# Hand-set TensorE order, V mixed a batch ahead, in-place channel results and GpSimd sorts in a fused attention and MLP kernel

## The chip, the cores and the metric

The kernel runs on one core of a Trainium2 chip. The metric is the time of one execution in microseconds (us), by the device's clock; several executions are timed and the median is given. A run is "fast" or "slow" by a simple rule: on one core it is called slow when it is more than 1.5% above the fastest of the same kernel. A ratio is the mean time of one kernel's fast runs over the mean of the other's fast runs of the same rounds, so it isn't quite the ratio of the medians quoted beside it.

The engines are TensorE (PE in the profile; its weight loads are PEld), VectorE (DVE), ScalarE (ACT), GpSimd (POOL) and SyncE (SP). In this kernel GpSimd issues the loads from DRAM, beside some elementwise work, and SyncE issues the stores, the V round trip through DRAM and the DMA transposes. In the traces here each of them works through its instructions in order: below, TensorE stands 7.5 us at one matmul with other work behind it.

## The reference, cut to what matters

Shapes: q, k, v are 4 batches x 8 heads x 768 x 64; the MLP's width is 512, hidden width 2048.

```python
P = sort_net                                  # (B, H, 8, 8)
for _ in range(5):                            # normalise rows, then columns
    P = exp(P - max(P)); P = P / sum_rows(P); P = P / sum_cols(P)
k_sorted = einsum('bhij,bhjcd->bhicd', P, k_blocks)   # "mixing" of K: 8 blocks of 96 rows
v_sorted = einsum('bhij,bhjcd->bhicd', P, v_blocks)   # "mixing" of V
x = softmax(q_b @ k_sorted_b^T / 8) @ v_sorted_b      # attention inside each block
a1  = alpha1 * x + beta1
tok = einsum('ts,bsd->btd', w_tok, a1)        # token mixing, 768 x 768
u   = x + lam * tok
ch  = relu((alpha2 * u + beta2) @ w_ch1) @ w_ch2      # hidden layer, then channel layer
out = u + lam * ch
```

## The kernel before

Per batch the kernel mixes K and V, does attention, the token layer (`tok`), the hidden layer (`h`) and the channel layer (`ch`). The MLP of one batch and the attention of the next are interleaved on TensorE. A scheduler sets the order of an engine's instructions unless `fixed` is set; `bufs` says how many copies of a tile exist. V takes a round trip: TensorE mixes it, the result is written to DRAM (`vscr`) and read back regrouped (`Vs`). W1 and W2 are the two MLP weights.

```python
# loads, issued by GpSimd (cut)
def load_weights():
    for g in range(4): pool.dma_start(W1p[...g...], w1v[...g...])
    load_raw(1, 1)                                    # V of batch 1
    for g in range(4): pool.dma_start(W2p[...g...], w2v[...g...])
...
def sort_wtok(n):                                     # regroups columns of w_tok
    for lo, hi, base in ((0, 96, 0), (96, 128, TAIL)):
        dve.tensor_copy(t_[:, :, :, lo:hi], wt16[...])
...
def emit_scores(b, h4, g, spins=0):                   # eight matmuls, then one exp
    sps = psa([128, 2, 4, 128], FT, "sc_ps")
    ...
def moe_ch(b, hf, kks=range(3)):
    ost = att.tile([128, C], FT, name="ost", tag="ost", bufs=2)
    ...
    dve.tensor_tensor(cps[:], cps[:], lamB[:, lo:hi], ALU.mult)
    dve.tensor_tensor(ost[:, lo:hi], cps[:], u_of[b][kt][:, lo:hi], ALU.add)
    nc.sync.dma_start(out[...], ost[...])
...
pool.tensor_copy(gate[:], Vs[1][0:1, 0, 0:2])         # "the Vs gate": GpSimd waits here
load_raw(2, 1)                                        # V of batch 2
load_raw(2, 0)                                        # K of batch 2
pool.fixed = False
...
for b in range(1, B):
    if b > 1:
        ...
        mixing_matrices(b); mix_v(b)                  # V of the batch itself
        ...
        mix_k(b)
    emit_attention(b)
    moe_h(b - 1, 0); moe_ch(b - 1, 0); moe_h(b - 1, 1) # (b > 1)
    moe_a(b)                                          # token layer and transposes of u
    moe_ch(b - 1, 1)
    if b == 1: load_q(2); cross_q(2)                  # q of batch 2 and its DMA transposes
```

The softmax here doesn't subtract the row's maximum and nothing guards it: scores larger than these inputs give would overflow.

## Time and profile before

| | before |
|---|---|
| median of the first 3 runs | 269.15 us (268.52 to 269.49); with a fourth, used in the comparison below, 268.94 |
| span of the profiled run | 266.8 us |
| TensorE busy | 257.6 us, 97% |
| first token matmul of batches 0, 1, 2, 3 | 34.1, 85.4, 144.2, 203.0 us |

The first lines are from the page of the profiled run: each engine's busy time, and (in 40 slices of the span) TensorE's busy tenths.

```profile
span 266.8 us, 5149 instructions
...
PE 257.6 (97%) x2049; PEld 141.6 (53%) x2059; DVE 154.8 (58%) x333; ACT 125.8 (47%) x232; POOL 92.5 (35%) x100
...
PE   7799999999999999999999999999999999999993
```

TensorE hardly idles from the second slice on, and the next view gives it the full clock (1.00) in every stretch. That view sums up stretches cut at the token layers; its columns are the stretch, its length, then busy time (and number of instructions) of PE, PEld, DVE, ACT and POOL, the granted clock, the DMA share and GB/s.

```profile
34.10:85.42 51.32, 51.12 (x442) 29.28 (x443) 36.38 (x72) 30.96 (x58) 26.77 (x28) 1.00 1.28 187
85.42:144.19 58.77, 58.46 (x418) 30.75 (x419) 35.10 (x71) 28.25 (x52) 25.52 (x25) 1.00 0.91 130
144.19:202.97 58.78, 58.47 (x419) 30.76 (x419) 35.11 (x71) 28.24 (x52) 16.42 (x13) 1.00 0.42 70
202.97:266.80 63.83, 59.53 (x321) 30.94 (x322) 22.84 (x40) 19.91 (x39) 4.00 (x4) 1.00 0.19 50
```

Two equal periods of 58.8 us stand between the token layers of batches 1, 2 and 3. In the chain of waits (start, length, what) one place in such a period isn't TensorE:

```profile
109.28 0.62 PE k_ps L65 x8
...
109.92 0.58 ACT kT L65
...
111.70 0.58 ACT kT L65
...
112.30 0.50 ACT hTa L65
```

Four evictions of mixed K on ScalarE, of which the first and the last are shown, hold the chain for 2.4 us. TensorE has other work meanwhile (a whole run of hidden matmuls), so most of it is hidden; "on the chain" means here only that the next hidden matmul group got its buffer from there.

### The profile page before, as it was taken

The page shows a single profiled execution, that of the slowest core. Times are in us where ns is not written, and L with a number is a line of the kernel's source. Part 1 is how long each engine was busy: PE and PEld are TensorE (multiplying, and loading weights), DVE is VectorE, ACT ScalarE, POOL GpSimd, SP SyncE. Part 2 cuts the span into 40 slices and gives each one's busy share as a digit, 9 for nine tenths or more (in the row PEclk, how much of TensorE's full clock was granted, in tenths as well). Part 3 has the DMA queues.
Part 4 walks back from the last instruction along what each step waited for, and adds up shares of the span by engine and source line. Part 5 has one row for each costly group of instructions (what it writes and reads, how often), then busy time and mean ns, then how long its engine had stood idle before and what let it go on. Part 6 is the DMA issues. An engine that isn't in the chain of part 4 may idle for free.

```text
span 266.8 us, 5149 instructions
## 1 busy us (share of the span) xinstructions
PE 257.6 (97%) x2049; PEld 141.6 (53%) x2059; DVE 154.8 (58%) x333; ACT 125.8 (47%) x232; POOL 92.5 (35%) x100
## 2 busy tenths in 40 slices
PE   7799999999999999999999999999999999999993
PEld 2467745565565444554565444554565445545542
DVE  5878788629567966722585966704675962042033
ACT  3376757643585312980375404970474305504600
POOL 8524689203575615007917225002409000000000
PEclk9999999999999999999999999999999999999999
DMA  6999999999999544499996342494200432012012
GB/s 83 174 208 251 207 210 207 211 216 112 211 157 155 113 84 117 114 82 89 202 211 136 61 100 80 118 98 62 80 2 2 81 76 79 2 39 79 2 39 79
DMA packets 62423, 30.88 MB, mean 116 GB/s; under 512 B 48888, under 2 KB 58112, under 8 KB 62400
## 3 DMA queue, kind: packets, MB, share of 16 engines
q0 software_dynamic: 23024, 15.60, 39.4%
q1 hardware_dynamic: 39280, 14.89, 32.6%
q8 instruction: 16, 0.26, 0.4%
q14 instruction: 7, 0.06, 0.1%
q10 hardware_dynamic: 96, 0.07, 0.1%
HBM read 32.78 MB, written 8.65 MB: 155 GB/s over the span
## 4 chain that ended last, share of the span: by engine, by line
PE 89%; ACT 4%; DVE 4%; issue 1%; DMA 1%; DVEq 0%; ACTq 0%
PE ch_ps L65 31%; PE h_ps L65 30%; PE tok_ps L65 12%; PE x_ps L65 5%; PE sc_ps L65 4%; ACT kT L65 2%; PE v_ps L65 2%; PE k_ps L65 1%; PE q_ps L65 1%; ACT et L65 1%; DVE csum L65 1%; DVE P L65 1%; PE m_ps L65 1%; DVE rsum L65 1%; DMA P<-in_sort_net_dram 1%
## 5 line engine op out<-in xcount | busy, mean ns | idle before, releaser
L65 PE MATMUL h_ps<-a2T,W1p 128*128 128x384 bf16 x512 | 93.4, 326 | 0.1
L65 ACT ACTIVATE hTa<-h_ps 128x384 bf16<-128x384 f32 x96 | 45.9, 492 | 68.1 <-PE h_ps L65 67.0
L65 PE MATMUL ch_ps<-W2p,hTa 128*128 128x512 bf16 (+2 forms) x290 | 65.9, 370 | 0.5
L65 PEld LDWEIGHTS <-W1p 128*128 128x128 bf16 x512 | 47.5, 98 | 30.3 <-issue 0.9
L65 DVE TENSOR_TENSOR ch_ps<-ch_ps,lamB 128x512 f32<-128x512 f32 (+2 forms) x25 | 16.9, 676 | 63.2 <-PE ch_ps L65 60.5
L65 POOL TENSOR_SCALAR u<-b1lB,rs 128x512 f32<-128x512 f32 x18 | 28.8, 1610 | 64.1 <-DVE ost L65 59.3
L65 PEld LDWEIGHTS <-hTa 128*128 128x128 bf16 x300 | 28.7, 98 | 32.4
L65 PE MATMUL tok_ps<-x,w_tokT 128*128 128x512 f16 x144 | 32.1, 379 | 0.0
L65 POOL TENSOR_TENSOR u<-x,u 128x512 f32<-128x512 f16 x22 | 25.3, 1181 | 18.1 <-DVE x L65 17.3
L65 ACT ACTIVATE et<-sc_ps 96x768 f16<-96x768 f32 x32 | 24.9, 807 | 11.7 <-PE sc_ps L65 11.7
L65 ACT CAST u<-u 128x512 f16<-128x512 f32 x24 | 14.8, 618 | 24.8 <-DVE u L65 24.8
L65 PE MATMUL ch_ps<-W2p,hTb 128*128 128x512 bf16 (+2 forms) x100 | 25.0, 371 | 0.0
L65 PEld LDWEIGHTS <-w_tokT 128*128 128x128 f16 x180 | 14.8, 97 | 16.1
L65 DVE TENSOR_TENSOR tok_ps<-tok_ps,a1lB 128x512 f32<-128x512 f32 x24 | 16.5, 692 | 7.3 <-PE tok_ps L65 7.3
L65 DVE CAST kT<-k_ps 64x512 f16<-64x512 f32 x24 | 16.5, 688 | 3.4 <-PE k_ps L65 3.0
L65 DVE TENSOR_TENSOR x<-x_ps,recip 96x512 f16<-96x512 f32 (+2 forms) x32 | 17.6, 554 | 0.9
L65 DVE TENSOR_TENSOR u<-tok_ps,u 128x512 f32<-128x512 f32 x24 | 16.4, 688 | 1.7
L65 ACT ACTIVATE hTb<-h_ps 128x384 bf16<-128x384 f32 x32 | 15.3, 497 | 3.8 <-PE h_ps L65 3.4
L65 DVE TENSOR_TENSOR ost<-ch_ps,u 128x512 f32<-128x512 f32 (+2 forms) x25 | 16.6, 665 | 0.6
L65 POOL DMA_DIRECT2D qn<-in_q_dram x18 | 15.5, 875 | 4.2 <-PE q_ps L65 3.4
L65 PEld LDWEIGHTS <-hTb 128*128 128x128 bf16 x100 | 9.6, 98 | 10.9
L65 PEld LDWEIGHTS <-et 96*128 96x128 f16 (+2 forms) x288 | 12.4, 99 | 4.6 <-issue 1.2
(95 smaller groups left out, 214.7 us busy)
## 6 DMA issues: line engine op xcount, KB each, us to landing
out_dram<-ost SPq DMA_DIRECT2D x23, 192.0 KB, 2.2
raw<-in_v_dram POOLq DMA_DIRECT2D x8, 384.0 KB, 8.9
raw<-in_k_dram POOLq DMA_DIRECT2D x8, 384.0 KB, 10.9
vscr<-vA SPq DMA_DIRECT2D x6, 384.0 KB, 4.4
Vs<-vscr SPq DMA_DIRECT2D x6, 384.0 KB, 7.7
W1p<-in_moe_w_ch_dram POOLq DMA_DIRECT2D x4, 512.0 KB, 10.1
W2p<-in_moe_w_ch_dram POOLq DMA_DIRECT2D x4, 512.0 KB, 17.9
qn<-in_q_dram POOLq DMA_DIRECT2D x12, 128.0 KB, 5.8
```

The lines of the kernel that those rows point to most:

```text
L65: ins = getattr(self.eng, name)(*args, **kwargs)
```

## The change

The intent: (1) from batch 1 TensorE's order is written out, with score groups in pairs and each attention step set after a stated amount of hidden and channel work; (2) V of batch b+1 is mixed during batch b; (3) the channel result is added into `u` in place, which frees memory; (4) the column sorts of w_tok go from VectorE to GpSimd; and the start of batch 0 is regrouped. With it the order of the loads changes. The core of the diff, with cuts:

```diff
 def sort_wtok(n):
-            dve.tensor_copy(
+            pool.tensor_copy(
                 t_[:, :, :, lo:hi], ...
... in moe_ch
-                dve.tensor_tensor(ost[:, lo:hi], cps[:], u_of[b][kt][:, lo:hi], ALU.add)
-                nc.sync.dma_start(out[...], ost[...])
+                dve.tensor_tensor(u32[:, lo:hi], cps[:], u32[:, lo:hi], ALU.add)
+                nc.sync.dma_start(out[...], u32[...])
... loads of batch 0 and 1
+    load_w1(range(2)); load_raw(1, 1)
+    for n in range(3):
+        sort_wtok(n)                      # GpSimd waits for w_tok here
+    load_w1(range(2, 3)); prep_affine(); load_raw(1, 0); load_w1(range(3, 4)); load_q(1)
...
+    load_w2(range(2))                     # first half of W2
...
-    pool.tensor_copy(gate[:], Vs[1][0:1, 0, 0:2])
-    load_raw(2, 1)
-    load_raw(2, 0)
-    pool.fixed = False
+    pool.tensor_copy(gate[32:64, :], Vs[1][32:64, 0, 0:2])
+    load_q(2)
+    load_w2(range(2, 4))                  # second half of W2, behind the gate
+    load_raw(2, 1)
+    load_raw(2, 0)
+    cross_q(2, regroup[1])                # six DMA transposes of q
+    moe_rows(1, range(5))
+    pe.fixed = True
...
     for b in range(1, B):
+        if b == 1:
+            fill = chain(moe_h(0, 1), moe_ch(0, 0), moe_ch(0, 1, (0,)))
+            steps = ...attention_steps(1, 3.0, 0.3)
+        else:
+            fill = chain(moe_h(b - 1, 0), moe_ch(b - 1, 0), moe_h(b - 1, 1), moe_ch(b - 1, 1, (0,)))
+            steps = ...mix_k..., attention_steps(b, 5.3)
+        if b < B - 1:                     # V of the next batch
+            steps[at:at] = [(g, lambda n=n: mixes(b + 1, n)) ...]
+        weave(fill, steps)                # a step follows so many us of fill
+        moe_a(b)
+        run(moe_ch(b - 1, 1, (1, 2)))
+        if b < B - 1:
+            moe_rows(b + 1, range(3))
+        if b == 1:
+            load_q(3); load_raw(3, 1); load_raw(3, 0); cross_q(3, turned[-1])
```

## The prediction

> **What bounds the kernel.** TensorE. The page gives PE 97% busy of 266.8 us, and the chain of waits is 89% PE. Busy is not issue time, so I read starts in that view: 64 hidden-layer matmuls (384 columns) take 10.40 us, 162.5 ns each; 36 token matmuls (512 columns) 7.77 us, 216 ns. That is N/2.4 GHz plus about 2.5 ns, as the Trainium skill states ("TensorE: Matmul & The Clock Gate", "Wait, 56ns, not 53.3ns?"), so these runs have no slack. By the chain, in stages:
> - 0 to 12 us: normalising P (DVE/ACT chain), TensorE spinning.
> - 12 to 34: batch 0 attention and turning w_tok; first token matmul at 34.1.
> - 34 to 55: token, hidden and V mixing of batch 0, nearly dense.
> - 55 to 93: batch 1. Then two equal periods of 58.8 us (93.4, 152.2, 211.0), then a dense 52 us to 262.4 and a 4 us tail.
>
> **A 58.8 us period.** Hidden, channel and token matmuls need 20.8 + 20.7 + 7.8 = 49.3 us, mixing V and K 2.8. Scores and values plus stalls take the other 6.7. Before runs eight score groups of eight matmuls (0.31 us each, of which about 0.13 is the switch out of it, plus 0.09 going in) and TensorE stands still 0.1 to 0.3 us at some hidden or score groups (timeline: K evictions of 4 x 0.58 us on ACT hold the chain).
>
> **What the change does.**
> 1. Fixed TensorE order with paired score groups (four of sixteen) placed among channel/hidden units so each evacuation is covered. It should save about 0.23 x 4 us of switching plus half of the stalls: 1.5 us in each of the two periods, 1 us in batch 1. The dense end is unchanged.
> 2. V mixed a batch ahead: mostly moved work (1.3 us a batch stays); it takes the Vs round trip through DRAM (4.4 + 7.7 us to land) off the start of each batch. Included in 1.
> 3. In-place channel result: same two DVE operations; frees memory for two hidden tiles and eleven u tiles. No time of its own.
> 4. Batch 0: K before V, q issued before the identity, ten spin matmuls in the attention removed, w_tok evictions split over ACT and DVE. Scores start near 14.5 instead of 17.8 us. But w_tok still lands near 22.5 (before: GpSimd's W1 issue waited for it until 23.06), and the sorts now follow it on GpSimd: DVE took 0.45 + 0.48 us per sort. GpSimd's cost for such a strided copy isn't in this trace; it takes 2.7 cycles per element for tensor_tensor. The skill ("GPSIMD Engine Reference", "Engine selection") calls one-input operations "roughly line-rate", no run yet shows it: estimate 1.3 to 2.6 us per sort, all three done at 27 to 31. ACT then needs six evictions of about 0.65 us. I expect the first token matmul at 31 to 33: 1 to 3 us gained, not the 4 that earlier scores would give.
>
> Sum: 1.5 + 1.5 + 1 + 2 + 0.5 (batch 0's MLP) = 6.5 us. All on the TensorE chain.
>
> **Prediction: 262.6 us, 8 in 10 between 258.5 and 266.5.** Faster by over 2%: 0.66; within 2%: 0.31; slower: 0.03.
>
> **Right if** the first token matmul is at 31 to 33 us, periods are about 57.3 us, score groups show as sixteen. **Wrong if** a GpSimd sort takes over 3.5 us (first token matmul at 35 or later); if the fixed order now waits in batch 1 for late loads (q of batch 1, W2's second half, V of batch 2), as W1, W2 and q were moved behind the sorts and the Vs gate; or if exp, evictions and relu saturate ACT where scores lie within hidden units. If w_tok sorting is cheap, the gain could reach 9 us.

## More of the kernel before

GpSimd's loads, in order of time (start, length of issuing, engine, operation, what, count, idle time before it and what ended it):

```profile
27.31 1.54 POOL L65 DMA_DIRECT2D W2p<-in_moe_w_ch_dram  x2
29.09 0.75 POOL L65 DMA_DIRECT2D W2p<-in_moe_w_ch_dram  x1 [0.24 <-DMA W1p<-in_moe_w_ch_dram]
31.60 0.74 POOL L65 DMA_DIRECT2D W2p<-in_moe_w_ch_dram  x1 [1.76 <-DMA W1p<-in_moe_w_ch_dram]
```

So all of W2 is issued by 31.6 us. By the completion counts in the trace it has landed by 50.2 us, and the channel layer first needs it at 55.2.

## The result, and the profile after

The changed kernel takes 279.4 us (median of 4 runs, 277.96 to 281.36) against 268.94 us before: ratio 1.0392, 95% interval 1.032 to 1.0465. It is 3.9% slower. The same lines of the page of the changed kernel:

```profile
span 279.6 us, 5126 instructions
...
PE 254.3 (91%) x2047; PEld 141.0 (50%) x2047; DVE 143.7 (51%) x313; ACT 138.6 (50%) x251; POOL 92.4 (33%) x100
...
PE   5988899999710999999999999999999999999994
...
PEclk9999899999975799999999999999999999999999
```

There is a hole at slices 11 to 13 (about 75 to 91 us) where TensorE is nearly idle, and the granted clock drops to half around it and once before, at slice 5. The stretches, cut at the token layers as before:

```profile
32.37:106.75 74.38, 59.68 (x467) 32.11 (x466) 34.38 (x70) 38.00 (x68) 28.26 (x32) 0.89 1.25 153
106.75:163.63 56.88, 56.53 (x420) 30.79 (x418) 32.46 (x62) 31.89 (x57) 23.87 (x23) 1.00 1.12 138
163.63:219.38 55.75, 55.39 (x414) 30.23 (x412) 31.75 (x62) 28.84 (x54) 16.08 (x13) 1.00 0.18 44
219.38:279.60 60.22, 56.24 (x309) 29.33 (x306) 22.84 (x40) 19.39 (x38) 5.96 (x6) 0.99 0.20 53
```

The two later periods went from 58.8 to 56.9 and 55.8 us; the stretch of batch 1 went from 51.3 to 74.4. Two pieces of work moved into that stretch from later ones: a third of a channel half (16 matmuls at 216 ns, 3.45 us, from the end) and one V mixing (6 x 216 ns, 1.3 us, out of the third period). That explains 4.75 of the 23.1 us. Most of the rest is told by TensorE's waits (what waited, for what: us in total, times, longest):

```profile
PE ch_ps L65 <- DMA W2p<-in_moe_w_ch_dram: 11.0, 2, 7.5
PE v_ps L65 <- DMA raw<-in_v_dram: 3.1, 1, 3.1
```

In the list of waits of the kernel before, no DMA appears for TensorE. In order of time:

```profile
75.06 0.38 PE L65 MATMUL ch_ps<-W2p,hT 128*128 128x512 bf16 x1
78.94 1.02 PE L65 MATMUL ch_ps<-W2p,hT 128*128 128x512 bf16 x4 [3.49 <-DMA W2p<-in_moe_w_ch_dram]
87.45 0.58 PE L65 MATMUL ch_ps<-W2p,hT 128*128 128x512 bf16 x1 [7.49 <-DMA W2p<-in_moe_w_ch_dram]
91.08 1.01 PE L65 MATMUL v_ps<-raw,bigV 128*128 128x512 f16 x2 [3.05 <-DMA raw<-in_v_dram]
```

TensorE runs one channel matmul at 75.06, then stands for the third and the fourth quarter of W2 and for V of batch 2: 3.5 + 7.5 + 3.1 = 14.0 us. While it stands the clock falls to half from 80.7 to 94.3 us (the trace's clock record). So the 23.1 us are 4.75 of moved work, 14.0 of stops, an estimated 1.6 for the work done at half clock from 91.1 to 94.3 us, 1.7 for another half-clock stretch at 32.9 us (see b2), and about 1 us that isn't accounted for. Why these loads are late, GpSimd shows:

```profile
24.64 4.67 POOL L65 COPY wtp<-wt 128x1152 f16<-128x1152 f16 x6 [6.39 <-DMA wt<-in_moe_w_tok_dram]
...
63.02 0.18 POOL L65 COPY gate<-Vs 32x2 f16<-32x2 f16 x1 [21.20 <-DMA Vs<-vscr]
63.62 5.26 POOL L65 DMA_DIRECT2D qn<-in_q_dram  x6 [0.42 <-issue]
68.82 1.55 POOL L65 DMA_DIRECT2D W2p<-in_moe_w_ch_dram  x2
70.29 1.16 POOL L65 DMA_DIRECT2D raw<-in_v_dram  x2
```

GpSimd's sorts took 4.67 us in all, well inside the estimate. But at the gate it waited 21.2 us until V of batch 1 had come back from DRAM, then issued q of batch 2, which is needed at about 134 us, and only then the second half of W2, needed at 75 us, and V of batch 2, needed soon after that. And beside these loads SyncE runs the six DMA transposes of that same q. A DMA transpose, undisturbed and queued one after another, starts 1.3 us after the one before it in the kernel before (first fence; one of the six came late because its u did); in the changed kernel (second fence) six hold SyncE for 24.5 us, of which only 0.4 us is waiting for q:

```profile
90.37 8.90 SPq L601 DMA_TRANSPOSE a2T<-u  x6
```

```profile
67.24 24.53 SPq L140 DMA_TRANSPOSE qT<-qn  x6
```

The loads suffer too: between 80 and 86 us all DMA together moved 98 GB/s. In e2 below, with the same loads and no transposes beside them, it moved 183 GB/s (69 to 77 us), so it isn't simply that more bytes had to be moved.

The kernel before had such an overlap as well, later on and with nobody waiting: five transposes of q of batch 3 beside loads of q, V and K took 12.9 us, where five of batch 2 had taken 7.2 us.

```profile
128.79 12.89 SPq L149 DMA_TRANSPOSE qT<-qn  x5
```

### The profile page after: what moved, and what is told of

It is laid out like the page before. It is cut to its first block, busy times and chain, and to the rows that moved or that the text cites. A ratio compares the mean times of both kernels' runs of the same rounds, so it can differ in the third digit from the quotient of the medians.

```text
span 279.6 us, 5126 instructions
## 1 busy us (share of the span) xinstructions
PE 254.3 (91%) x2047; PEld 141.0 (50%) x2047; DVE 143.7 (51%) x313; ACT 138.6 (50%) x251; POOL 92.4 (33%) x100
## 4 chain that ended last, share of the span: by engine, by line
PE 67%; DMA 20%; POOL 6%; ACT 3%; DVE 1%; issue 1%; SPq 0%; POOLq 0%; DVEq 0%
PE ch_ps L65 29%; PE h_ps L65 21%; PE tok_ps L65 11%; DMA raw<-in_v_dram 7%; DMA wt<-in_moe_w_tok_dram 6%; DMA Vs<-vscr 4%; DMA vscr<-vA 3%; POOL qn L65 2%; PE x_ps L65 2%; PE v_ps L65 2%; ACT kT L65 2%; PE sc_ps L65 2%; POOL wtp L65 2%; POOL raw L65 1%; ACT hT L65 1%
## 5 line engine op out<-in xcount | busy, mean ns | idle before, releaser
L65 PE MATMUL ch_ps<-W2p,hT 128*128 128x512 bf16 (+2 forms) x400 | 89.0, 374 | 11.0 <-DMA W2p<-in_moe_w_ch_dram 11.0
L65 PE MATMUL h_ps<-a2T,W1p 128*128 128x384 bf16 x512 | 89.5, 326 | 1.4 <-ACT hT L65 0.7
L65 ACT ACTIVATE hT<-h_ps 128x384 bf16<-128x384 f32 x128 | 60.3, 493 | 53.4 <-PE h_ps L65 53.0
L65 PEld LDWEIGHTS <-hT 128*128 128x128 bf16 x400 | 38.0, 99 | 46.0 <-issue 5.4
L65 DVE TENSOR_TENSOR ch_ps<-ch_ps,lamB 128x512 f32<-128x512 f32 (+2 forms) x25 | 16.9, 676 | 74.1 <-PE ch_ps L65 51.4
L65 PE MATMUL tok_ps<-x,w_tokT 128*128 128x512 f16 x144 | 33.9, 393 | 0.0
L65 ACT CAST u<-u 128x512 f16<-128x512 f32 x24 | 14.7, 618 | 28.0 <-DVE u L65 28.0
L65 DVE RECIPROCAL recip<-x_ps 96x8 f32<-96x8 f32 (+1 forms) x32 | 6.2, 195 | 28.8 <-PE x_ps L65 28.8
L65 ACT CAST vA<-v_ps 128x1024 f16<-128x1024 f32 x8 | 8.1, 1010 | 21.5 <-PE v_ps L65 21.5
L65 DVE TENSOR_TENSOR u<-ch_ps,u 128x512 f32<-128x512 f32 (+2 forms) x25 | 16.7, 667 | 0.8
L65 PEld LDWEIGHTS <-et 96*128 96x128 f16 (+1 forms) x288 | 12.1, 105 | 2.3
L65 PE MATMUL x_ps<-Vs,et 96*128 96x65 f16 (+1 forms) x288 | 12.6, 197 | 0.0
## 6 DMA issues: line engine op xcount, KB each, us to landing
W2p<-in_moe_w_ch_dram POOLq DMA_DIRECT2D x4, 512.0 KB, 13.3
```

What stands on the lines that cost most here:

```text
L65: ins = getattr(self.eng, name)(*args, **kwargs)
```

## The experiments

Theories, as they stood after reading the traces. A: loads that miss a deadline. B: GpSimd's sorts push all later loads back. C: the hand-set order costs time in itself. D: DMA transposes and loads that run side by side slow each other. E: mixing V a batch ahead, which moves a deadline forward, is the main cost. Every kernel below gave correct outputs. "Landing" is read from the completion counts of a DMA in the trace.

### e1: all of W2 early

```diff
     moe_start(0)
-    load_w2(range(2))
+    load_w2(range(4))
...
     load_q(2)
-    load_w2(range(2, 4))
     load_raw(2, 1)
```

> Only edit to the changed kernel: the second half of W2 is issued together with the first half (at about 41 us), not behind GpSimd's wait for Vs of batch 1. Theory A (late loads: what GpSimd issues behind the Vs gate at 63 us misses its deadline, and a hand-set TensorE order turns that into a stop): both W2 waits (3.5 and 7.5 us) vanish, only a wait for V of batch 2 at about 77 us remains, no longer than 5 us; time 266 to 271 us. Theory B (GpSimd sorts are to blame) and theory C (the hand-set order itself costs time everywhere): little moves, above 276 us.

Measured: 275.41 us (273.04 to 277.38), ratio 1.02 (1.0138 to 1.0262), outside the range I gave. The W2 waits are gone, as theory A has it. But the profile, which fell on the run that counts as slow (277.38), has two V waits:

```profile
PE v_ps L65 <- DMA raw<-in_v_dram: 7.3, 2, 4.2
```

The first, 4.2 us, is V of batch 2 as expected. The second is V of batch 3, at 130 us: in the changed kernel the earlier stop had hidden that it is late too. While it was loaded, SyncE again ran transposes of q:

```profile
120.59 16.85 SPq L140 DMA_TRANSPOSE qT<-qn  x3
```

Three transposes took 16.9 us. So a delay taken away early turned up again at the next deadline, and taking away 11.0 us of W2 waits bought about 5 us (from 3.9% to 2.0% over the kernel before, fast runs).

### e2: the transposes of q of batch 2 a phase later

```diff
     load_raw(2, 0)
-    cross_q(2, regroup[1])
...
         if b == 1:
+            cross_q(2, turned[-1])
             load_q(3)
```

> Only edit: the six DMA transposes of q of batch 2, which run from 67 to 92 us beside the late loads and are not needed before about 134 us, are issued after the transposes of u of batch 1. If they choke the loads (theory D): W2's second half lands by about 80 and V of batch 2 by about 83 us instead of 87 and 91, time 269 to 274 us. If the loads are only late because they are issued late (theory A alone): landing times move by less than 2 us, time above 277 us.

Measured: 288.38 us (283.29 to 291.1; two of the four runs count as slow), ratio of the fast runs 1.0745. The landing times moved as theory D said: W2's last quarter at 77.6 instead of 87.4 us, V of batch 2 at 81.3 instead of 90.9 (2.4 us of it because the gate opened earlier). From issue to landing the last W2 quarter took 10.4 us instead of 17.8. But the time got worse: q of batch 3 has to wait for the transposes of q of batch 2 (they share a buffer), V of batch 3 stands behind q of batch 3 in GpSimd's queue, and TensorE stood 9.6 us for it (and 3.0 us for W2):

```profile
PE v_ps L65 <- DMA raw<-in_v_dram: 13.1, 2, 9.6
```

So D is supported by the landings; that the whole loss lies in this place is not.

### e3: sorts on VectorE, each before its pair of transposes

```diff
-            pool.tensor_copy(
+            dve.tensor_copy(
                 t_[:, :, :, lo:hi], ...
-    for n in range(3):
-        sort_wtok(n)
     load_w1(range(2, 3))
...
+    sort_wtok(0)
     prep_wtok(range(0, 2))
     pv0(3, 0)
+    sort_wtok(1)
     prep_wtok(range(2, 4))
     ...
```

> Only edit: the three sorts of w_tok run on VectorE again (each just before its pair of transposes), so GpSimd's queue never waits for w_tok. Theory B (GpSimd sorts delay all later loads and so cause the stop): the stop in batch 1 shrinks by over 6 us and the time is below 273 us. Theory A: the DMA queue was never empty until 55 us, so loads land as before; only the first token matmul comes 1 to 2.5 us earlier and the half-clock stretch at 33 us may go; time 275 to 279 us.

Measured: 283.18 us (280.7 to 288.61), ratio 1.0487: a miss, in the direction against theory B. The first token matmul came at 40.1 us instead of 32.2, since sort, transposes, evictions and the next sort had become one serial chain:

```profile
PE wtok_ps L65 <- DVE wtp L65: 5.1, 3, 2.2
PE ch_ps L65 <- DMA W2p<-in_moe_w_ch_dram: 3.9, 2, 3.6
```

W1's third quarter, which stood behind the sorts, was issued 5 us sooner and landed no sooner (38.8 instead of 38.0 us): the DMA queues had been busy all the time. The last quarter of W2 and V of batch 2 landed no sooner either (87.8 and 91.8 us instead of 87.4 and 90.9). With 3.5 us for V the stops in batch 1 came to 7.4 us instead of 14.0, a fall that theory B had asked for; but from the token layer on TensorE's work came 7.8 us later here, and that alone brings it closer to loads that land as before.

### e5: V mixed in its own batch

```diff
-        if b < B - 1:
-            at = len(steps) - (3 if b == 1 else 6)
-            steps[at:at] = [(g, lambda n=n: mixes(b + 1, n)) ...]
...
+            steps = [(g, lambda n=n: mixes(b, n)) for n, g in enumerate((0.6, 0.7, 1.1))]
```

> Only edit: V of batches 2 and 3 is mixed at the start of its own batch, no longer a batch ahead. If the V deadline moved ahead is the main cause (theory E): time 268 us or less. Theory A: the W2 waits stay (W2's second half still lands at 79 and 87 us), only the 3 us wait for V goes: 274 to 278 us.

Measured: 295.31 us (293.32 to 297.42), ratio 1.0969: far outside what I expected, and slower than the changed kernel. The W2 waits stayed (5.8 us) and the V wait went, as A has it, but the later batches now waited for the Vs round trip (4.0 us in batch 2) and, with the fill used up, for VectorE before the token layer (6.1 us in two waits). The edit changed where the fill ends as well, so it doesn't measure V's mixing ahead by itself. It shows no sign that E is the main cause. But E has a part in the V wait: before, TensorE first reads V of batch 2 at 106 us, in the changed kernel it would at about 77.

### b1: loads in the order of their deadlines

All W2 at 41 us; behind the gate V and K of batch 2, then q; V and K of batch 3 after the rows of u; transposes of q a phase later.

```diff
-    load_q(2)
-    load_w2(range(2, 4))
     load_raw(2, 1)
     load_raw(2, 0)
-    cross_q(2, regroup[1])
+    load_q(2)
     moe_rows(1, range(5))
+    load_raw(3, 1)
+    load_raw(3, 0)
...
         if b == 1:
-            load_q(3); load_raw(3, 1); load_raw(3, 0); cross_q(3, turned[-1])
+            cross_q(2, turned[-1]); load_q(3)
+        if b == 2:
+            cross_q(3, turned[-1])
```

> The changed kernel with its loads put in the order of their deadlines: all of W2 at 41 us, behind the Vs gate V and K of batch 2 first and q after them, V and K of batch 3 right after the u rows of batch 1, and the transposes of q a phase later. Theory A+D (late loads, made later by transposes running beside them, are the whole loss): no wait of TensorE for W2 or V over 1 us in any batch, last matmul near 256 to 259 us, time 261 to 265 us, 2 to 3% faster than before. If the hand-set order or the GpSimd sorts cost by themselves (B, C): above 268 us.

Measured: 269.9 us (269.14 to 270.21), ratio 1.0026 (0.9988 to 1.0063). About 9.8 of the 10.5 lost us are back (0.26% of 269 us, 0.7 us, is left) and no load makes TensorE wait any more, but the time is not the expected 261 to 265 us. One new wait is left:

```profile
PE h_ps L65 <- DVE a2T L65: 4.1, 1, 4.1
```

It is the hidden layer of batch 1, waiting for transposed u. SyncE's queue shows why:

```profile
85.50 11.12 SPq L364 DMA_DIRECT2D Vs<-vscr  x2
96.71 3.54 SPq L716 DMA_DIRECT2D out_dram<-u  x1
...
101.83 7.85 SPq L648 DMA_TRANSPOSE a2T<-u  x6
```

V and K of batch 3, issued at 83 us, ran beside the read of Vs of batch 2; SyncE was held for 11.1 us in issuing that read, the stores and the transposes of u behind it came late, and the stop was followed by 6.8 us at half clock.

### b2: b1 with ten spin matmuls between the w_tok transposes

```diff
+    spin(psa([128, 512], FT, "spin_ps")[:], 3)
     prep_wtok(range(2, 4))
     ...                                   # 3 more before the last pair, 4 after
```

> As b1, with ten spin matmuls between the w_tok transposes where TensorE waits for GpSimd's sorts and the evictions. If the half-clock stretch of 3.4 us at 33 us came from that idling, it is gone in the profile and the time is 1 to 2 us below b1; if the clock there has another cause, the stretch stays and the time is 0 to 1 us above b1.

Measured: 270.44 us (269.65 to 272.0), ratio 1.0057. Inconclusive: the half-clock stretch at 33 us was in neither profile, b1's or b2's, so there was nothing to remove; the first token matmul came 1.4 us later. Whether the 3.4 us stretch in the changed kernel (1.7 us lost: 18 token matmuls took 5.59 us by its chain, against 3.91) came from idling there stays open.

### b3: b1 with all three sorts on VectorE, together

> As b1, with the three sorts on VectorE, all three together ahead of the first w_tok transpose (in e3 each sat in front of its own pair and the chain became serial, first token matmul at 40 us). Sorts on GpSimd take 4.7 us in all from 24.6 us; on VectorE about 1.8 us, but behind the batch 0 work. If the sort's engine matters to the start, the first token matmul moves by over 1.5 us from 32.3; I expect within 1 us, and the time within 1.5 us of b1.

The edit is that of e3, with the three calls together ahead of the first `prep_wtok`. Measured: 272.52 us (271.33 to 274.81), ratio 1.0137. The first token matmul came at 35.5 us instead of 32.2; I had expected no more than 1 us. TensorE waited once for the sorts:

```profile
PE wtok_ps L65 <- DVE wtp L65: 2.9, 1, 2.9
```

Each sort is shorter on VectorE (0.6 us for a pair of copies in most of e3's and 1.6 us on GpSimd), but VectorE gets to it only after batch 0's work. The time is 2.6 us above b1, outside the 1.5 us I gave. Theory B falls: GpSimd is the better place here.

### b4: b1 with the transposes of q where the changed kernel has them

> As b1, but the transposes of q of batches 2 and 3 at the places where the changed kernel has them. If transposes beside loads are harmful only where a load is about to be needed (A with D), V of batch 2 lands before 76 us all the same, no stop of over 1 us, and the time is within 1.5 us of b1. If they hurt by themselves: over 3 us above b1.

```diff
     load_q(2)
+    cross_q(2, regroup[1])
     ...
-            cross_q(2, turned[-1]); load_q(3)
+            load_q(3); cross_q(3, turned[-1])
```

Measured: 278.7 us (277.76 to 279.95), ratio 1.0354: nearly all of the loss is back with no late load. The waiting goes a way that I had not thought of. GpSimd first, then VectorE:

```profile
97.19 1.56 POOL L65 TENSOR_SCALAR u<-b1lB,rs 128x512 f32<-128x512 f32 x1 [13.15 <-DMA out_dram<-u]
```

```profile
99.91 0.69 DVE L65 TENSOR_TENSOR u<-tok_ps,u 128x512 f32<-128x512 f32 x1 [7.46 <-POOL u L65]
```

The transposes (77.4 to 86.9 us) stood in SyncE's queue ahead of the stores of the output, and the loads of batch 3 ran beside these stores. Since the channel result is now in place, a buffer of u is free only when its store is done; GpSimd waited 13.2 us for that before it could make the last row of the next u, VectorE waited for GpSimd, and TensorE stopped 5.2 us in the middle of the token layer (and 4.9 us later on). So the in-place result has a cost where stores are late. How much of b4's loss is due to the transposes and how much to the loads of batch 3 beside the stores, this run doesn't separate.

### b5: V and K of batch 3 later

```diff
     moe_rows(1, range(5))
-    load_raw(3, 1)
-    load_raw(3, 0)
...
         if b == 1:
+            load_raw(3, 1); load_raw(3, 0)
             cross_q(2, turned[-1]); load_q(3)
```

> As b1, but V and K of batch 3 are issued where the changed kernel has them (after the last u rows of the next batch, about 106 us), ahead of q of batch 3. In b1 their early loads ran beside the Vs round trip of batch 2, held the Sync queue for 10.8 us and made the transposes of u 5 us late (4.1 us TensorE wait and 6.8 us at half clock). Theory A+D: that stop is gone, V of batch 3 lands by about 117 us before its use near 121, no TensorE wait over 1 us after 33 us, time 261 to 264 us: the prediction's number. If another cause remains: above 266 us.

Measured: 275.41, 275.48, 273.09 and 264.7 us. The first three are slow and there is one fast timing, so no ratio. No result is taken from them. The one profile (275.41, a slow run) shows VectorE waiting 9.9 us for the transposes of u; the granted clocks (0.981, 0.981, 0.984; 1.0 in the run of 264.7) would fit that in all three:

```profile
116.35 1.25 DVE L65 TENSOR_SCALAR a2T<-a2T,ab2col 128x384 bf16<-128x384 f16 x4 [9.92 <-DMA a2T<-u]
```

The last of these transposes was issued at 102.4 us, just when the loads began (101.9). Whether it gets through before them may decide the run. That isn't shown: the run of 264.7 us has no profile.

### b6: the same loads one GpSimd group earlier

> As b5, but V and K of batch 3 are issued one GpSimd group earlier (about 95 us, before the u rows that in-place results make wait for output DMAs). They then run beside the transposes of u that the hidden layer needs at 103 us. If transposes beside loads are slow (D): transposes of u slow from 1.2 to over 2 us each and a stop of 1 to 5 us returns before the hidden layer, time 263 to 269 us. If not: same as b5 within 0.7 us.

The edit moves the two `load_raw(3, ...)` of b5 ahead of `moe_rows(2, range(3))`. Measured: 271.05 us (270.12 to 271.45), ratio 1.0052. The loads were issued at 95.3 us; the transposes of u took 13.3 us instead of 7.9, and TensorE waited 4.5 us for them, as theory D had it (its range was 263 to 269, so the time was a miss by 2 us):

```profile
94.47 13.31 SPq L648 DMA_TRANSPOSE a2T<-u  x6
```

### b8: no load beside a transpose

```diff
     load_w2(range(4))                     # as e1
...
+    moe_rows(1, range(5))                 # ahead of the gate
     pool.tensor_copy(gate[32:64, :], Vs[1][32:64, 0, 0:2])
-    load_q(2); load_w2(range(2, 4)); load_raw(2, 1); load_raw(2, 0)
-    cross_q(2, regroup[1]); moe_rows(1, range(5))
+    load_raw(2, 1); load_raw(3, 1); load_q(2); load_raw(2, 0)
...
         if b == 1:
-            load_q(3); load_raw(3, 1); load_raw(3, 0); cross_q(3, turned[-1])
+            cross_q(2, turned[-1]); load_q(3); load_raw(3, 0)
+        if b == 2:
+            cross_q(3, turned[-1])
```

> Changed kernel with loads ordered by deadline and kept apart from every DMA transpose: W2 whole at 41 us, the u rows of batch 1 ahead of the Vs gate, behind the gate V of batch 2, V of batch 3, q of batch 2, K of batch 2 (all landed by about 84 us, before the Vs trip of batch 2 at 86 and the transposes of u at 94), K of batch 3 after q of batch 3. b1, b4, b5 and b6 each lost 4 to 9 us where K and V loads ran beside transposes or the Vs trip; the one b5 timing of 264.7 us shows what is left without it. Theory A+D: transposes of u take 1.2 us each and land on time, no TensorE wait over 1 us after 33 us, all timings (not only one) within 261 to 265 us, 2 to 3% under before. If the hand-set order costs by itself: above 267 us.

Measured over five rounds: 265.59 us (265.01 to 266.81, six runs), ratio 0.9893 (0.9864 to 0.9923). All runs lie together, no longer in two groups. The time is just above the 261 to 265 us that I expected, and the gain is 1.1%, not 2 to 3%. The transposes take their plain time, and TensorE's longest wait after 33 us is 0.7 us:

```profile
97.19 7.85 SPq L648 DMA_TRANSPOSE a2T<-u  x6
...
106.68 7.81 SPq L140 DMA_TRANSPOSE qT<-qn  x6
```

```profile
PE h_ps L65 <- DVE u L65: 1.0, 2, 0.7
```

### c1 and c2: the order given back to the scheduler

```diff
     moe_rows(1, range(5))                 # in c2: load_raw(2, 0)
-    pe.fixed = True
+    pe.fixed = False
```

> The changed kernel with TensorE's order left to the scheduler from batch 1 on (its stream then differs only in where the K mixing of batches 2 and 3 and four channel matmuls stand). Theory A+D: [...]the scheduler knows nothing of late loads and puts the channel matmuls and V mixing at the same places: stops for W2 and V of 10 to 16 us as in the changed kernel, time 276 to 283 us. Theory C (the hand-set order causes the stop): below 272 us.

> b8 with TensorE's order left to the scheduler from batch 1 on. If fixing the order is worth little beyond the interleaving written in the program: time within 1.5 us of b8 (265.6). If fixing it is what shortened the periods: over 268 us. If it costs time: below 264 us.

c1 (the changed kernel with a free order): 279.52 us (276.54 to 283.15; two of the four runs count as slow), ratio 1.0386, the same as the changed kernel within the noise. Its stops are the same two kinds, in the profile of its fastest run (276.54), where they come to 6.9 us, under the 10 to 16 I expected:

```profile
PE ch_ps L65 <- DMA W2p<-in_moe_w_ch_dram: 4.9, 1, 4.9
...
PE v_ps L65 <- DMA raw<-in_v_dram: 2.0, 2, 1.7
```

c2 (b8 with a free order): 264.65 us (263.86 to 265.93), ratio 0.9838 (0.9785 to 0.9892). It is the fastest of all, 1.6% under the kernel before; 0.9 us from b8, with ranges that overlap, so I don't call the difference shown. Left free, the scheduler keeps the interleaving that the program states but for the K mixing and four channel matmuls, so c1 and c2 test little more than the flag. Theory C falls by b8: it has the hand-set order and no stop. No run tried the changed loads with the order of the kernel before. c2's stretches, to be held against those of before:

```profile
32.90:89.27 56.37, 55.43 (x464) 31.36 (x466) 33.28 (x68) 37.99 (x68) 28.24 (x32) 1.00 1.18 193
89.27:146.15 56.88, 56.26 (x415) 30.81 (x418) 31.55 (x62) 31.89 (x57) 23.11 (x21) 1.00 0.98 130
146.15:201.90 55.75, 55.18 (x410) 30.22 (x412) 31.75 (x62) 28.84 (x54) 16.08 (x13) 1.00 0.25 58
201.90:262.10 60.20, 56.08 (x306) 29.34 (x306) 22.85 (x40) 19.39 (x38) 5.96 (x6) 0.99 0.21 53
```

## Why the prediction was wrong, point by point

The prediction said 262.6 us, 258.5 to 266.5; measured were 279.4. The chance given to "slower by over 2%" was 0.03.

- **What bounds the kernel: right.** TensorE; the start-to-start times of N/2.4 GHz + 2.5 ns, as the Trainium skill has it ("TensorE: Matmul & The Clock Gate", "Wait — 56ns, not 53.3ns?"), held before and after: 36 token matmuls take 7.77 us in both.
- **The start: right.** Scores at 14.4 us (14.5 predicted), first token matmul at 32.2 (31 to 33; the stretches above are cut at 32.37, where the matmul before it ends). w_tok landed at 24.6, not 22.5, and the sorts took 4.67 us in all, 1.6 us each, near the low end of 1.3 to 2.6: that the two balanced is luck. The skill ("GPSIMD Engine Reference", "Engine selection") calls one-input operations "roughly line-rate". Here that was 1.0 ns for each of the 4608 elements of a partition; it doesn't mean as fast as VectorE, which took 0.6 to 1.0 us for such a sort in the kernel before. What I had missed there is the half-clock stretch at 32.9 us, which took back 1.7 us in this run.
- **The two periods: right, a little better than predicted.** 57.3 predicted; 56.9 with equal work, and 55.8 + 1.3 for the V mixing that moved out = 57.1. Score groups stand as sixteen. The flag that fixes the order isn't needed for it: c2, with a free order, has the same periods. How much came from the paired groups and how much from shorter stalls wasn't measured.
- **Batch 1: this step failed.** The prediction has "1 us in batch 1" of gain, V ahead "Included in 1" as moved work, and "All on the TensorE chain": it gave the moved loads no wait on that chain. In the page of the changed kernel DMA has 20% of the chain, against 1% before. Measured were 14.0 us of TensorE stops, an estimated 1.6 us more from half clock between 91.1 and 94.3 us (3.2 us at half speed), and no gain underneath: c2, where no load is late, needs 56.4 us for this stretch against 51.3 + 4.75 = 56.1 for the same work before. The batch 0 gain of 0.5 us isn't there either.
- **The risk was named and not costed.** "If the fixed order now waits in batch 1 for late loads (q of batch 1, W2's second half, V of batch 2)" is what happened, for two of the three. The numbers for a sum were in the trace of before: GpSimd's gate opened when V had come back from DRAM, W2's quarters landed 2.5 us apart at the rate that the queue then had, six loads of q take about 0.9 us each to issue. My estimate from these, made afterwards: a gate at 63 us, 5.3 us of issuing q, two quarters of W2 at 2.5 us and two halves of V at about 1.9 us come to some 77 us for V, just when it is needed, with nothing to spare. That would have been warning enough, and it is still too kind: in e2, with no transposes beside the loads and the gate 2.4 us earlier, W2 had landed at 77.6 us and V at 81.3. What the sum leaves out is D: beside transposes the same loads landed about 10 us later than in e2 (2.4 us of it the gate). Of D the trace of before had a sign that I overlooked, the five transposes that took 12.9 us; its loads of V there were not slow (7.2 and 8.9 us to land), so the size of D couldn't be read from it.
- **Sum of what is real.** c2's last matmul starts at 257.9 us against 262.4 before: 1.2 us from the start, 1.9 and 1.7 from the periods, 0.3 lost in batch 1. That is 4.5 of the predicted 6.5 us. The rest of the difference between 265 and 279 us is when loads, transposes and rows of u are issued: the changed kernel and b8, and c1 and c2, differ in nothing else.

What is shown: late W2 and V make the stop (e1 removes the one wait, b1 all of them); the order and the sorts don't (b8; e3, b3); transposes and loads side by side slow each other (e2, b6). What is argued only: why they do. It isn't peculiar to transposes: in b1 the read of Vs, no transpose, took 14.7 us to land beside loads, against 6.5 us in b8. The skill ("DMA: Bandwidth & Descriptors", "Queues, rings and completion order") says that a DMA engine takes turns between its queues packet by packet. In the changed kernel the trace fits: the transposes' packets have 256 bytes, those of W2 1024 and those of V 6144 (473 ns or more each), and the two queues' packets came about one for one (912 and 918 between 76 and 88 us, 4-byte completion records counted). In other overlaps they didn't (153 and 523 in e1 between 124 and 130 us), and whether a record of the trace is what the page calls a packet isn't shown. No run changed a packet's size, so it stays an explanation.

## What to carry to other kernels

When work is moved ahead, move its loads first: write down for each load when it is issued, how many us the queue needs for what stands before it, and when it is used, and do so again after each repair, since the next deadline in line becomes the stop. Keep loads and DMA transposes that something waits for in different stretches of time. An in-place result saves a buffer, but it ties the reuse of that buffer to the store, so a queue that is late with stores then holds up engines that had nothing to do with them.

## What the Trainium skill lacked or had wrong

- "DMA: Bandwidth & Descriptors", "Rules for kernel authors", says that a transpose next to ordinary DMAs needs nothing. That holds for correctness in all runs here, but not for time: six transposes took 24.5 us beside loads of W2 and V against 7.8 us alone, and the loads were slowed too (the last W2 quarter took 17.8 us to land, 10.4 us without the transposes beside it).
- The same page's account of taking turns by packets has no number for a queue of small packets beside one of large packets. Here three transposes beside loads with 6144-byte packets took 16.9 us (about 4 us alone).
- "TensorE: Matmul & The Clock Gate" on the clock gate agrees: half-clock stretches here, but for those cut off by the kernel's end, were 3.4, 6.8, 10.2 or 13.7 us, whole multiples of its 3.4 us window. One of them began at 32.9 us with no wait over 0.4 us in the ten us before; b4, b5 and c1 had it too and b1, e2 and b6 didn't, with the same code up to there. What sets it off stays open.
- "GPSIMD Engine Reference" gives no time for a `tensor_copy`. Here 6 copies of 16-bit elements in runs of 96 or 32, with 4608 elements per partition in all, took 4.67 us.
